# Attention with an MLP behind it: loads of two head pairs in one transfer, rests in eight, a start from two queues, and a new order

## The chip, the cores and the metric

The kernel runs on one core of one Trainium2 chip. The metric is the device time of one execution in microseconds (us), the median of several runs. A kernel under test and the kernel before run in the same rounds on the same chip. A ratio is the mean time of one kernel's fast runs over the mean time of the other's fast runs of the same rounds, so it is not quite the ratio of the medians quoted beside it. A span in a profile is about 2 us shorter than the time of its run.

## The reference, cut to what matters

```python
# q, k, v: (8 batches, 12 heads, 448 tokens, 64), f32
q_n, k_n = rmsnorm(q, g_q), rmsnorm(k, g_k)
attn = softmax(q_n @ k_n.T / sqrt(64)) @ v          # per batch and head
x = attn.transpose(0, 2, 1, 3).reshape(3584, 768)
h = x @ w_in                                        # 768 x 2048
out = (h * clip(h + 3, 0, 6) / 6) @ w_out           # 2048 x 768
```

448 tokens are three tiles of 128 and a rest of 64. Two heads make a pair; a batch has six pairs and there are 48 in all.

## The kernel before

The program first collects all its operations in a list, with the engines that may do each, and then emits them in a fixed order, a table of numbers found by a search. Each engine works through its own instructions strictly in that order. TensorE (PE) does the scores, the values and both matmuls of the MLP; the MLP of one batch fills PE while the attention of the next goes through its chain. SyncE (SP) issues the loads of q, k and v, the transposes done by DMA (`T` of q and k, `xT` of the attention's output) and the stores of the result. The weights are issued by GpSimd (POOL).

The parts that the change touches: loads are issued for each pair, and the 64-token rests for two pairs at a time.

```python
NQK, NV, NVR, ..., NY = 5, 5, 2, ..., 3              # buffers in each ring
qk_r = ring(NQK, [TP, 2 * FULL + 4 * D], FP32, "qk") # q and k of one pair and the rests of two
...
def load(P, want, parts="kqRrvw"):                   # P: the pair
    ...
        if c in "kqv":                               # 128 x 2 heads x 192: 192 KB
            em(nc.sync.dma_start(
                out=dst.rearrange("p (h x) -> p h x", h=2),
                in_=src[b, hs, 0:T * TP].rearrange("h (p t) d -> p h (t d)", t=T)))
        ...
        for n in range(2):                           # even pairs: R (q), r (k), w (v), 64 x 2 x 64: 32 KB
            em(nc.sync.dma_start(out=dst, in_=rows))
...
if P >= NPT:                                         # 13: from here q and k are transposed by DMA, before by PE
    em(nc.sync.dma_start_transpose(out=dst[...], in_=qks[...]))
```

The softmax here doesn't subtract the row's maximum and nothing guards it: scores larger than these inputs give would overflow.

## Time and profile before

| | kernel before |
|---|---|
| time, median (lowest to highest) | 462.8 us (462.6 to 463.7) |
| span in the profile | 461.1 us |
| PE busy / idle | 423.9 / 37.2 us |
| PE idle before 60, in 100 to 260, in the rest | 15.1 / 17.2 / 4.9 us |
| issues of loads of q, k and v | 288 |

The table is read from the windows that the prediction shows: a stretch's length less PE's busy time in it is PE's idle time, and only PE's idle time or a low clock can be gained, because PE is the fullest engine. The prediction mentions the list of PE's waits in the third stretch without showing it. Here it is; the columns are the instruction's line, what it waited for, the sum in us, how often, and the longest.

```profile
PE X L715 <- ACT eT L680: 3.6, 3, 2.0
PE S L690 <- ACT eT L680: 2.7, 4, 1.5
PE M L769 <- DVE gT L786: 2.1, 2, 2.0
PE X L670 <- DVE xn L732: 2.0, 3, 0.8
PE M L769 <- DMA xT<-xn: 1.7, 2, 1.0
PE M L806 <- DVE gT L786: 1.6, 2, 1.5
PE M L769 <- ACT y L816: 1.1, 2, 0.7
```

Nearly every line names ScalarE (ACT) or VectorE (DVE), and none names SP. The chain of waits, whole span:

```profile
PE 48%; DMA 7%; SPq 4%; DVE 3%; POOL 2%; ACT 1%; issue 1%; ACTq 0%; POOLq 0%; DVEq 0%
```

There the transfers and SP's queue follow PE, ahead of DVE and ACT.

### The profile page before, as it was taken

The page shows a single profiled execution, that of the slowest core. Times are in us where ns is not written, and L with a number is a line of the kernel's source. Part 1 is how long each engine was busy: PE and PEld are TensorE (multiplying, and loading weights), DVE is VectorE, ACT ScalarE, POOL GpSimd, SP SyncE. Part 2 cuts the span into 40 slices and gives each one's busy share as a digit, 9 for nine tenths or more (in the row PEclk, how much of TensorE's full clock was granted, in tenths as well). Part 3 has the DMA queues.
Part 4 walks back from the last instruction along what each step waited for, and adds up shares of the span by engine and source line. Part 5 has one row for each costly group of instructions (what it writes and reads, how often), then busy time and mean ns, then how long its engine had stood idle before and what let it go on. Part 6 is the DMA issues. An engine that isn't in the chain of part 4 may idle for free.

```text
span 461.1 us, 9700 instructions
## 1 busy us (share of the span) xinstructions
PE 423.9 (92%) x3629; PEld 246.4 (53%) x3629; DVE 279.5 (61%) x644; ACT 253.6 (55%) x486; POOL 161.8 (35%) x264
## 2 busy tenths in 40 slices
PE   8486899999889897999898999999999999999996
PEld 8243655554544454554454555555555565555554
DVE  5479587458687565866675477675568645345130
ACT  3488677768866654457665856664463433312110
POOL 4456863096464454462633333134040000000000
PEclk9769799999999999899999999999999999999999
DMA  6888999757866767677789767755144411120112
GB/s 163 175 167 181 238 222 225 185 158 193 152 140 151 190 147 197 143 167 200 189 156 192 193 154 144 138 151 146 32 99 96 94 47 31 29 80 1 68 36 103
DMA packets 123699, 64.25 MB, mean 139 GB/s; under 512 B 77828, under 2 KB 120196, under 8 KB 123652
## 3 DMA queue, kind: packets, MB, share of 16 engines
q1 hardware_dynamic: 118256, 57.24, 51.4%
q0 software_dynamic: 5248, 6.29, 8.7%
q8 instruction: 28, 0.46, 0.4%
q14 instruction: 19, 0.16, 0.1%
q10 hardware_dynamic: 148, 0.10, 0.1%
HBM read 45.61 MB, written 11.01 MB: 123 GB/s over the span
## 4 chain that ended last, share of the span: by engine, by line
PE 48%; DMA 7%; SPq 4%; DVE 3%; POOL 2%; ACT 1%; issue 1%; ACTq 0%; POOLq 0%; DVEq 0%
PE M L806 17%; PE M L769 15%; PE X L715 4%; PE S L806 4%; DMA qk<-in_k_dram 3%; DMA qk<-in_q_dram 2%; PE S L670 2%; PE X L769 1%; SPq L457 1%; SPq L602 1%; POOL sq L488 1%; PE S L769 1%; ACT eT L680 1%; DMA T<-qko 1%; SPq L438 1%
## 5 line engine op out<-in xcount | busy, mean ns | idle before, releaser
L769 PE MATMUL M<-xT,w_in_sb 128*128 128x448 bf16 x714 | 156.8, 355 | 5.7 <-DVE gT L786 2.3
L806 PE MATMUL M<-w_out_sb,gT 128*128 128x384 bf16 x752 | 136.9, 326 | 1.6 <-DVE gT L786 1.6
L680 ACT ACTIVATE eT<-S 128x896 bf16<-128x896 f32 x114 | 102.0, 915 | 41.3 <-PE S L670 41.1
L806 PEld LDWEIGHTS <-gT 128*128 128x128 bf16 x912 | 86.3, 98 | 62.9 <-issue 10.1
L769 PEld LDWEIGHTS <-w_in_sb 128*128 128x128 bf16 x768 | 71.3, 98 | 73.3 <-issue 19.1
L786 DVE SCALAR_TENSOR_TENSOR gT<-ts,M 128x448 bf16<-128x448 f32 x119 | 73.5, 619 | 33.5 <-ACT ts L780 30.9
L495 DVE TENSOR_REDUCE ssq<-sq 128x12 f32<-128x768 f32 (+4 forms) x51 | 52.3, 1027 | 33.1 <-POOL sq L488 24.5
L488 POOL TENSOR_TENSOR sq<-qk 128x384 f32<-128x384 f32 (+2 forms) x49 | 44.7, 917 | 64.6 <-DMA qk<-in_q_dram 26.2
L715 PEld LDWEIGHTS <-eT 128*128 128x128 bf16 x1152 | 45.8, 99 | 22.5 <-issue 7.0
L782 DVE TENSOR_SCALAR ts<-M 128x448 f32<-128x448 f32 x73 | 45.2, 621 | 18.4 <-PE M L769 18.1
L715 PE MATMUL X<-va,eT 128*128 128x65 bf16 x1152 | 49.5, 196 | 6.2 <-ACT eT L680 3.9
L486 ACT ACTIVATE sq<-qk 128x384 f32<-128x384 f32 (+1 forms) x48 | 27.5, 574 | 36.9 <-DMA qk<-in_q_dram 21.6
L528 POOL TENSOR_TENSOR qke<-qk,rs 128x384 bf16<-128x384 f32 x45 | 36.8, 825 | 26.5 <-ACT rs L503 20.4
L780 ACT ACTIVATE ts<-M 128x448 f32<-128x448 f32 x46 | 25.0, 546 | 38.2 <-PE M L769 37.3
L528 POOL TENSOR_TENSOR qko<-qk,rs 128x384 bf16<-128x384 f32 x44 | 35.6, 827 | 17.5 <-DMA T<-qko 8.4
L670 PE MATMUL S<-T 64*128 64x448 bf16 x228 | 35.3, 372 | 2.7 <-ACT eT L680 1.9
L732 DVE TENSOR_TENSOR xn<-X,rd 128x512 bf16<-128x512 f32 x48 | 33.2, 691 | 5.1 <-DMA xT<-xn 3.2
L819 DVE TENSOR_SCALAR y<-M 128x384 f32<-128x384 f32 x27 | 14.9, 553 | 26.7 <-PE M L806 26.6
L694 ACT ACTIVATE eR<-S 128x448 bf16<-128x448 f32 x48 | 26.4, 550 | 6.7 <-PE S L690 6.7
L680 ACT ACTIVATE eT<-X 128x896 bf16<-128x896 f32 x30 | 27.4, 915 | 0.0
L670 PEld LDWEIGHTS <-T 64*128 64x128 bf16 x288 | 11.1, 94 | 26.9 <-issue 19.9
L399 POOL CAST va<-vf 128x384 bf16<-128x384 f32 x19 | 9.6, 503 | 42.8 <-PE X L715 22.0
(84 smaller groups left out, 351.2 us busy)
## 6 DMA issues: line engine op xcount, KB each, us to landing
qk<-in_k_dram SPq DMA_DIRECT2D x48, 192.0 KB, 2.8
qk<-in_q_dram SPq DMA_DIRECT2D x48, 192.0 KB, 3.2
vf<-in_v_dram SPq DMA_DIRECT2D x48, 192.0 KB, 3.1
out_dram<-y SPq DMA_DIRECT2D x23, 384.0 KB, 2.5
w_in_sb<-in_moe_w_in_dram POOLq DMA_DIRECT2D x4, 768.0 KB, 9.8
w_out_sb<-in_moe_w_out_dram POOLq DMA_DIRECT2D x4, 768.0 KB, 8.5
out_dram<-y SPq DMA_DIRECT2D x9, 192.0 KB, 2.8
qk<-in_q_dram SPq DMA_DIRECT2D x48, 32.0 KB, 2.8
```

Of the source, the lines that this page charges most:

```text
L486: em(nc.scalar.square(out=o, in_=x))
L488: em(nc.gpsimd.tensor_tensor(out=o, in0=x, in1=x, op=A_MULT))
L495: em(nc.vector.tensor_reduce(out=ssq[:, c0:c1], in_=sq[:, c0 * D:c1 * D].rearrange("p (n d) -> p n d", d=D), axis=AX_X, op=A_ADD))
L528: em(nc.gpsimd.tensor_tensor(out=qks[:, b0:b0 + T].rearrange("p t h d -> p h t d"), in0=x, in1=rs[:, c0:c0 + 2 * T].rearrange("p (h t) -> ...
L670: em(nc.tensor.matmul(out=ps[:, a, 0:S], lhsT=qkT[r, k0:k0 + TP], rhs=qkT[r, q0:q0 + S], start=True, stop=True))
L680: em(nc.scalar.activation(out=eT[:, t, PAD:PAD + S2].rearrange("p (a s) -> p a s", a=2), in_=ps[:, :, 0:S], func=EXP, bias=0.0, scale=1.0))
L715: em(nc.tensor.matmul(out=X_ps[:, i // 2, o:o + (E1 if t < T else 2 * E1)], lhsT=eT[:, t, c0:c0 + TP] if t < T else eR[:, c0:c0 + TP], rhs ...
L732: em(nc.vector.tensor_tensor(out=xn[:].rearrange("p (a i) h d -> p a (i h) d", a=2), in0=xv[:, :, :, 0:D], in1=rd[:].unsqueeze(3).to_broad ...
L769: em(nc.tensor.matmul(out=ps[:, 0:S], lhsT=w_in_sb[:, kt, f * 128:(f + 1) * 128], rhs=xT[:, kt, x0:x0 + S], start=(kt == 0), stop=(kt == N ...
L782: em(nc.vector.tensor_scalar(ts[:], ps[:, 0:S], -3.0, 3.0, A_MAX, A_MIN))
L786: em(nc.vector.scalar_tensor_tensor(out=gT[:, f, e * S:(e + 1) * S], in0=ts[:], scalar=lim, in1=ps[:, 0:S], op0=op, op1=A_MULT))
L806: em(nc.tensor.matmul(out=ps[:, 0:nc0], lhsT=gT[:, f, i * 128:(i + 1) * 128], rhs=w_out_sb[:, f, c0:c0 + nc0], start=(f == 0), stop=(f == ...
```

## The change

Its intent is to take issues off SP: q of two pairs comes in one transfer of 384 KB, and so do k and v; the rests of a whole batch come in eight transfers (four for q, two each for k and v) instead of eighteen. The buffers are cut to match: three double ones for six pairs, and two for y instead of three. At the start, q of the first pair and the first rests go out from ACT's queue while SP sends k. Two more pairs are transposed by DMA, and the order and the choice of engines were searched again. The core of the diff:

```diff
-    NQK, NV, NVR, ..., NY = 5, 5, 2, ..., 3
-    qk_r = ring(NQK, [TP, 2 * FULL + 4 * D], FP32, "qk")
+    NQK, NRR, ..., NY = 3, 2, ..., 2
+    qk_r = ring(NQK, [TP, 2, 2, FULL], FP32, "qk")
+    rr_r = ring(NRR, [TP, 2, H // 2, D], FP32, "rr")
 ...
-    NPT = 13
+    NPT = 11
 ...
+    def load(P, want, parts="kqv", n=1, first=False):
+            def fn(e, dst=dst, src=src):
+                em((nc.scalar if e == ACT else nc.sync).dma_start(
+                    out=dst.rearrange("p o (h x) -> p (o h) x", h=2),
+                    in_=src[b, hs, 0:T * TP].rearrange("h (p t) d -> p h (t d)", t=T)))
+    def load_rest(b, want, parts, m0, m1, first=False):
+        ...                                     # R: four transfers, r and w: two each, for pairs m0 to m1
+                em((nc.scalar if e == ACT else nc.sync).dma_start(out=dst, in_=rows))
 ...
+    load(0, -70.0, "q", first=True)             # first=True: from ACT's queue
+    load_rest(0, -69.0, "Rr", 0, 1, True)
+    load(0, -70.0, "k")
 ...
-            load(P + 4, at(P + 4) - 30.0)
+            elif P % 2 == 0:
+                load(P + 4, at(P + 4) - 30.0, n=2)
+            if (P + 4) % NPAIR == 0:
+                load_rest((P + 4) // NPAIR, at(P + 4) - 30.0, "Rrw", 0, NPAIR // 2)
 ...                                            # ORDER (2349 numbers) and the choice of engines: new
```

## The prediction

> **What bounds the kernel now.** I began with the page's busy shares. PE works 92% of the span, so a gain has to come from PE's idle time or from low-clock time, and I cut the span into stages by windows.
>
> ```profile
> PE 423.9 (92%) x3629; PEld 246.4 (53%) x3629; DVE 279.5 (61%) x644; ACT 253.6 (55%) x486; POOL 161.8 (35%) x264
> ...
> 0.00:60.00 60.00, 44.89 (x468) 31.25 (x469) 39.46 (x158) 37.07 (x76) 35.02 (x71) 0.83 0.87 185
> 60.00:100.00 40.00, 38.93 (x344) 22.37 (x342) 25.02 (x53) 29.89 (x61) 17.79 (x27) 1.00 0.87 189
> 100.00:260.00 160.00, 142.85 (x1266) 79.00 (x1266) 108.82 (x226) 103.42 (x207) 82.15 (x123) 0.99 0.75 173
> 260.00:300.00 40.00, 39.81 (x347) 22.65 (x344) 27.01 (x56) 26.01 (x51) 11.80 (x18) 1.00 0.74 158
> 300.00:420.00 120.00, 120.00 (x976) 68.39 (x974) 69.64 (x138) 49.80 (x77) 15.00 (x26) 1.00 0.31 77
> 420.00:461.00 41.00, 37.44 (x240) 22.73 (x237) 9.56 (x16) 7.46 (x15) 0.00 (x0) 1.00 0.17 59
> ```
>
> Columns: stretch, its length, busy us of PE, PEld, DVE, ACT, POOL, granted clock, DMA share, GB/s. PE idles 15.1 us before 60 (part of the rest at a clock of 0.83), 1.1 in 60 to 100, 17.2 in 100 to 260, 0.2 in 260 to 300, nothing in 300 to 420, 3.6 in the tail: 37 in all. Only the first and the third stretch have something to give.
>
> For the third I asked what PE waits for. Its list has no big item (exponentials 6.8 us, xn 2.9, gT 3.7, a transposed xT 1.7), and neither ACT (65%) nor DVE (68%) is full. So I looked at what feeds them, the queue of SP, which the page does not count as an engine.
>
> ```profile
> 112.73 0.61 SPq L457 DMA_DIRECT2D vr<-in_v_dram  x1
> 113.39 0.59 SPq L438 DMA_DIRECT2D qk<-in_q_dram  x1
> 114.03 0.61 SPq L457 DMA_DIRECT2D qk<-in_q_dram  x1
> 114.68 1.30 SPq L602 DMA_TRANSPOSE T<-qko  x1
> 116.15 1.29 SPq L602 DMA_TRANSPOSE T<-qke  x1
> 117.48 0.66 SPq L438 DMA_DIRECT2D vf<-in_v_dram  x1
> 118.19 0.63 SPq L457 DMA_DIRECT2D qk<-in_k_dram  x1
> 118.92 0.91 SPq L457 DMA_DIRECT2D qk<-in_q_dram  x1
> 119.93 1.23 SPq L739 DMA_TRANSPOSE xT<-xn  x1
> ```
>
> Start and length of each issue: one begins as the last ends. Adding up these lengths over all of 100 to 260 gives 150 of 160 us (37.0, 38.2, 37.3, 37.3 in the four quarters), against 22.5 of 40 in 60 to 100 and 32.4 of 40 in 260 to 300. PE is idle where SP is full, and hardly elsewhere. SP issues in order: a transpose that PE needs stands behind loads that nobody needs yet, and the reverse. The chain of waits runs through just that: issue, transfer, square, reduction, issue.
>
> ```profile
> 168.38 0.63 SPq L457
> 169.07 0.59 SPq L830
> 169.70 0.60 SPq L457
> 170.35 2.16 DMA qk<-in_k_dram
> 172.58 1.05 POOL sq L488
> 173.65 1.23 DVE ssq L495
> ```
>
> The start is another stage. PE first stalls on the 64-row rest of k (pair 0), whose loads stood tenth and thirteenth in the queue. Its real work starts at 19.8.
>
> ```profile
> 19.11 0.40 PE L633 MATMUL M<-identity,qke 128*128 128x128 bf16 x2 [3.48 <-POOL qke L554]
> ```
>
> From the first exponential at 20.4 to the end of the sixth pair's last one at 49.1, ACT sets the pace: I count 26.9 us of its instructions in these 28.7 us (17 exponentials of 128x896 at 0.915 and six of 128x448 at 0.55 alone are 18.9). The MLP's matmuls, the filler that makes PE full, begin at 53.
>
> **The Trainium skill.** "DMA: Bandwidth & Descriptors", section Issuing engines are not separate DMA queues, says that issuing from several engines saves only the sequencer's time to start the transfers, "usually small relative to the DMA itself". One issue here is small (0.6 us against 2.8 to 3.2 to landing), but 197 of them in a row fill 94% of SP. "Perfetto Trace Analysis", section DMA Instruction — HWDGE, says that the length shown is the wait for the descriptor generator, its use and the sequencer's semaphore push, not the movement of data. So the lengths above are SP's own occupancy, and fewer issues free it even if all bytes stay. "TensorE: Matmul & The Clock Gate", Part 1, says that the array falls to half clock after an idle window of about 3.4 us and needs as long a busy one to come back. The trace agrees: after the stall of 3.48 us the granted clock is 0.50 from 18 to 30.
>
> **The change part by part.** Loads on SP: six pairs now take 18 of 192 KB (0.53 us each) and 18 of 32 KB (0.62): 9.5 + 11.2 = 20.7 us. Afterwards 9 of 384 KB and 8 rest transfers. If the length of an issue depends little on its size, that is 9 x 0.53 + 8 x 0.62 = 9.7 us. This is an estimate; for it speaks that 64x2x64, with 128 runs, takes 0.62 and 128x2x192, with 256 runs, 0.53. In 100 to 260 there are 149 load issues; 17/36 of them is 70, so 79 x 0.57 = 45 us leave SP, and its 150 become 105, or 71% of a shorter stage: between the 56% and 81% of the two neighbours, which lost 1.1 and 0.2 us. At 1.1 per 40 us, the 17.2 of idle become 4.3, a gain of 12.9. But PE's own list names ACT and DVE, whose work the change does not reduce. Some of those gaps are theirs whatever SP does, so I count 11.
>
> The start: q of pair 0 and the rests of q and k go out from ACT while SP sends the two k. In the order of instructions the first scores stand before the k rest, so the 3.48 us stall leaves the path of the first score, and part of the dummy matmuls stands between the first scores and should hold the clock. With the data landed by about 7 and the known steps after it (reduction 0.7, two rs 0.4, scaling about 2, transposing and copying 1.2) the first exponential comes at about 13, an estimate. But ACT then has to work off 36.3 us of instructions up to the sixth pair's last exponential (32.4 before, counted in both orders with the durations of this trace), of which 4.8 are done by then: 13 + 31.5 x 28.7/26.9 = 46.6 against 49.1. Seven microseconds of earlier start shrink to 2.5. Some of ACT's extra (one exponential of 0.9, casts) is later work done early, so I count 3.
>
> PE: 15 fewer transposes (99 to 84, as pairs 11 and 12 go to DMA) at about 0.1 us each: 1.5, on the path because PE is full. For it SP has two more issues of 1.3. PE's other counts are the same: 768 + 912 MLP matmuls, 1344 for the values.
>
> Added and off the path: even pairs from the second on take three squares instead of two; 58 of 825 ns and 14 smaller ones make POOL's squares about 56 us instead of 45, on an engine that is 51% busy in the full stage. ACT's fall from 27.5 to 24. One y buffer less: a row block of y takes PE 32 x 0.163 = 5.2 us and its store lands after about 3, so two suffice. Bytes and run lengths stay, so the DMA share stays near 0.75. Sum: 11 + 3 + 1.5 = 15.5, so 462.8 becomes 447.3.
>
> **The rivals.** First, ACT and DVE are the real bound of 100 to 260. PE's list speaks for it, and the new order pulls pairs 10 to 18 forward with less filler (I count 44.5 us of PE, 46.6 of ACT, 44.9 of DVE). Against: before, the same pairs took 54.9 us from exponential to exponential though no engine had over 48.5 of work, while SP was full. If it holds, the stage gives 5 and the time is about 454. Second, an issue's length grows with what it carries: 384 KB then cost 1.06 and the large rests up to three times 0.62. SP would get back some 30 of its 45 us, the gain would be 4 and the time 455. The equal lengths of unequal forms speak against it. Third, larger transfers land later, and one awaited piece now waits for twice its bytes; with buffers for six pairs of inputs that should be covered, but where it isn't it costs some 3 us at the start: 450. Fourth, the searched order fits the chip better than I count, the start keeps its seven and the stage loses its 17 nearly whole: 440.
>
> **Range and chances.** The central sum is 447.3. The fourth rival sets the lower edge at 440, the first and half the second the upper at 454.5. Faster by over 2% means under 453.6; only the first two rivals, near their full size, keep it above: 0.81. Same 0.17. Slower needs a new stall of over 9 us beside a freed SP: 0.02.
>
> **What would show it.** SP's lengths in about 100 to 250 should fall to some 70%, with double loads at 0.5 to 0.7 each. PE's idle there should be 4 to 8 us and the gaps named after xT gone. The first exponential should stand near 13, the sixth pair's last near 47, the clock before 60 above 0.83. PE's transposes should be 84. I am wrong if SP is free and PE still idles 12 us or more (first rival), if double loads show over 0.9 us (second), or if PE waits for transfers of q and k before 60 (third).

## The result, and the profile after

The changed kernel took 439.38 us (438.18 to 440.0, 4 runs) against 462.75 for the kernel before in the same rounds: ratio 0.9487, 95% interval 0.9464 to 0.9511. That is faster, as the prediction thought likely, but 8 us faster than its central value and just below the lower edge of its range.

The changed kernel's page and windows (stretch, length, busy us of PE, PEld, DVE, ACT, POOL, granted clock, DMA share, GB/s):

```profile
PE 416.4 (95%) x3614; PEld 241.3 (55%) x3614; DVE 277.8 (63%) x644; ACT 248.0 (57%) x484; POOL 171.2 (39%) x287
...
0.00:60.00 60.00, 43.65 (x489) 30.14 (x490) 38.56 (x159) 41.19 (x89) 38.86 (x79) 0.89 0.95 215
60.00:100.00 40.00, 38.88 (x358) 21.78 (x356) 28.89 (x65) 28.55 (x61) 18.93 (x31) 1.00 0.92 209
100.00:260.00 160.00, 159.76 (x1402) 88.59 (x1401) 123.70 (x252) 110.66 (x222) 91.52 (x140) 1.00 0.83 187
```

PE is idle for 0.24 us of the 160 from 100 to 260, where it was idle for 17.15. Its idle time over the whole span fell from 37.2 to 21.2. PE's list of waits for that stretch has one line left, and the chain of waits has neither DMA nor SP:

```profile
PE M L786 <- DVE gT L803: 0.2, 1, 0.2
```

```profile
PE 82%; DVE 7%; ACT 2%; issue 1%; DVEq 0%; ACTq 0%
```

SP's own queue in the changed kernel has gaps by the second half of the stretch (start, length of the issue), where it had stood end to end before:

```profile
195.22 1.96 SPq L619 DMA_TRANSPOSE T<-qke  x1
197.23 1.29 SPq L619 DMA_TRANSPOSE T<-qko  x1
198.75 1.19 SPq L756 DMA_TRANSPOSE xT<-xn  x1
203.29 0.36 SPq L847 DMA_DIRECT2D out_dram<-y  x1
203.76 1.32 SPq L619 DMA_TRANSPOSE T<-qke  x1
```

In these lines no load stands between the transposes, and SP stands idle from 200 to 203.3.

The spans differ by 461.1 - 437.6 = 23.5 us. Of these 16.0 are PE's idle time (16.9 less in 100 to 260, 1.2 more before 60, 0.3 less elsewhere) and 7.5 are PE's busy time. The fifteen transposes that left PE are about 1.5 of the 7.5, at the prediction's 0.1 us each. In 180 to 220 the clock rose from 0.96 to 1.00, which is 0.04 x 40 = 1.6. The rest, some 4, I put down to the higher clock before 60 (0.83 to 0.89) without having measured it apart.

### The profile page after: what moved, and what is told of

Same layout as the page of the kernel before. It is cut to its first block, busy times and chain, and to the rows that moved or that the text cites. A ratio compares the mean times of both kernels' runs of the same rounds, so it can differ in the third digit from the quotient of the medians.

```text
span 437.6 us, 9478 instructions
## 1 busy us (share of the span) xinstructions
PE 416.4 (95%) x3614; PEld 241.3 (55%) x3614; DVE 277.8 (63%) x644; ACT 248.0 (57%) x484; POOL 171.2 (39%) x287
## 2 busy tenths in 40 slices
DMA packets 123377, 64.71 MB, mean 148 GB/s; under 512 B 77508, under 2 KB 119876, under 8 KB 123332
## 4 chain that ended last, share of the span: by engine, by line
PE 82%; DVE 7%; ACT 2%; issue 1%; DVEq 0%; ACTq 0%
PE M L786 29%; PE M L823 27%; PE X L732 9%; PE S L687 6%; PE S L823 5%; PE S L707 2%; DVE gT L803 2%; DVE ssq L512 1%; DVE xn L749 1%; ACT eT L697 1%; DVE ts L799 1%; PE X L823 1%; PE X L687 1%; PE X L786 1%; PE X L766 1%
## 5 line engine op out<-in xcount | busy, mean ns | idle before, releaser
L697 ACT ACTIVATE eT<-S 128x896 bf16<-128x896 f32 x124 | 110.8, 917 | 44.7 <-PE S L687 39.4
L799 DVE TENSOR_SCALAR ts<-M 128x448 f32<-128x448 f32 x69 | 42.9, 622 | 36.3 <-PE M L786 34.1
L502 POOL TENSOR_TENSOR sq<-qk 128x384 f32<-128x384 f32 x58 | 47.3, 824 | 31.0 <-DVE ssq L512 13.1
L732 PEld LDWEIGHTS <-eT 128*128 128x128 bf16 x1152 | 47.6, 100 | 13.9 <-issue 2.2
L797 ACT ACTIVATE ts<-M 128x448 f32<-128x448 f32 x50 | 27.3, 546 | 37.6 <-PE M L786 29.6
L687 PE MATMUL S<-T 64*128 64x448 bf16 x248 | 38.0, 365 | 3.0 <-DVE T L606 1.6
L833 ACT ACTIVATE y<-M 128x384 f32<-128x384 f32 x24 | 11.8, 490 | 36.2 <-PE M L823 36.0
L836 DVE TENSOR_SCALAR y<-M 128x384 f32<-128x384 f32 x23 | 12.8, 555 | 29.9 <-PE M L823 29.9
L500 ACT ACTIVATE sq<-qk 128x384 f32<-128x384 f32 x38 | 19.4, 522 | 7.6 <-DMA qk<-in_k_dram 4.1
L823 PE MATMUL S<-w_out_sb,gT 128*128 128x384 bf16 (+1 forms) x128 | 22.1, 316 | 0.1
```

The costliest lines, as they stand in the source:

```text
L502: em(nc.gpsimd.tensor_tensor(out=o, in0=src, in1=src, op=A_MULT))
L687: em(nc.tensor.matmul(out=ps[:, a, 0:S], lhsT=qkT[r, k0:k0 + TP], rhs=qkT[r, q0:q0 + S], start=True, stop=True))
L697: em(nc.scalar.activation(out=eT[:, t, PAD:PAD + S2].rearrange("p (a s) -> p a s", a=2), in_=ps[:, :, 0:S], func=EXP, bias=0.0, scale=1.0))
L732: em(nc.tensor.matmul(out=X_ps[:, i // 2, o:o + (E1 if t < T else 2 * E1)], lhsT=eT[:, t, c0:c0 + TP] if t < T else eR[:, c0:c0 + TP], rhs ...
L797: em(nc.scalar.activation(out=ts[:], in_=ps[:, 0:S], func=RELU, bias=3.0, scale=1.0))
L799: em(nc.vector.tensor_scalar(ts[:], ps[:, 0:S], -3.0, 3.0, A_MAX, A_MIN))
```

## The experiments

Two theories stood. **A**: SP's occupancy by issues makes PE idle, so anything that takes issues off SP gains, and the names ACT and DVE in PE's list are only who stood last in a chain that SP had delayed. **B**: something else in the change does it: the larger transfers themselves, or the new order, which could have removed the idle time without the merging. Later the number of small transfers, apart from the time that their issues take of SP, joined B.

### Splitting the loads again, in the new order

In the changed kernel, every merged load is sent as single-pair transfers, at its place in the order (only the rests of q stay at four a batch). `e1_split_all` splits both kinds, `e2_split_big` only the first block, `e3_split_rest` only the second.

```diff
-                em((...).dma_start(out=dst.rearrange("p o (h x) -> p (o h) x", h=2), in_=...))
+                for i in range(n):
+                    em((...).dma_start(out=dst[:, i].rearrange("p (h x) -> p h x", h=2), in_=...[pair i]))
 ...
-                    em((...).dma_start(out=dst, in_=rows))
+                    for i in range(1 if c == "R" else m1 - m0):
+                        d, s = (dst, rows) if c == "R" else (dst[:, 2 * i:2 * i + 2], rows[:, 2 * i:2 * i + 2])
+                        em((...).dma_start(out=d, in_=s))
```

> The changed kernel with its order, but every merged load split again at its place: 34 load issues for six pairs instead of 17 (before had 36). Theory A (fewer issues free SP, and that removed PE's idle time): the idle time between 100 and 240 comes back by 10 us or more, and the time is 452 to 462. Theory B (the new order removed it, the merging is secondary): within 3 us of the changed kernel, 437 to 442.

> Only the transfers of two pairs of heads are split (18 + 8 issues for six pairs). A: nine more issues of 0.5 us in six pairs, about a half of the loss of the full split, 443 to 451. B: within 3 us of the changed kernel.

> Only the 64-row rests of k and v are split, by head pairs (9 + 16 issues). A: eight more issues of 0.6 us, again about half of the loss, 443 to 451. B: within 3 us of the changed kernel.

Measured: all split 470.78 us (ratio to before 1.0149, interval 1.0104 to 1.0194); only the large ones 444.9 (0.9591; median of its three fast runs, the fourth was slow); only the rests 459.81 (0.9907). Theory A had the direction right and the sizes wrong: 470.8 and 459.8 lie above the ranges that it gave (452 to 462, 443 to 451). The new order without the merging is slower than the kernel before, so the order alone is not the gain; it needs a short queue on SP. The chain of waits of the run with all split, and its list of PE's waits in 140 to 260:

```profile
PE 50%; SPq 12%; DMA 11%; POOL 11%; DVE 7%; issue 5%; ACT 2%; POOLq 0%; DVEq 0%; ACTq 0%
```

```profile
PE S L690 <- DVE T L607: 6.7, 1, 6.7
PE M L789 <- DMA xT<-xn: 5.8, 2, 5.5
```

SP's queue is now second in the chain, and the first wait is put down to DVE although it is a transposed tile that DVE could only scale once SP had issued its transpose:

```profile
152.53 1.91 SPq L466 DMA_DIRECT2D vr<-in_v_dram  x3
154.47 0.60 SPq L466 DMA_DIRECT2D rr<-in_q_dram  x1
155.18 1.32 SPq L622 DMA_TRANSPOSE T<-qke  x1
```

```profile
159.58 0.93 PE L690 MATMUL S<-T 64*128 64x448 bf16 x4 [6.70 <-DVE T L607]
```

The last write to qke had ended at 142.5. From 144.7 to 155.1 SP sent fifteen issues of loads end to end, then this transpose, which landed at 158.6. That is how the names in PE's list mislead.

Splitting the rests costs 20 us and splitting the large loads about 5.5, though they add nearly the same number of issues (8 and 9 a batch). The rests' issues are longer, and in the middle they add 27 us to SP's time, the large loads' 21 (table below). A split rest also goes out as a burst of three issues (six where both halves follow each other), and I suppose that such a burst in front of a transpose costs more than pairs of issues do. That was not tested.

### Merging the loads in the old order

`e4_old_order_merged` has the changed kernel's loads and buffers, but the order and the choice of engines of the kernel before, mapped operation by operation; a merged load stands where the first of its parts stood, or later where its buffer isn't free. The first loads are those of the kernel before, all on SP. With three y buffers it doesn't fit the memory, so it has two. `e4c_before_two_y` is its control: the kernel before with two y buffers and nothing else.

```diff
-NQK, ..., NY = 5, ..., 3        # e4c: this line alone
+NQK, ..., NY = 5, ..., 2
```

> The kernel before, in its own order, way choices and first loads, with the merged transfers from the fifth pair of head pairs on (a merged load stands where the first of its parts stood, or as early as its buffer allows; two y buffers). A: the idle time of 17 us in 100 to 260 falls to 4 to 6, time 447 to 452. B: it stays above 12 us, time 457 to 464.

> The kernel before with two y buffers instead of three and nothing else. This is a control for the run that merges the loads in the old order, which also had to lose a y buffer. If two buffers suffice, as the prediction said: 462 to 465 us, within 0.5% of the kernel before. If the store of y holds its buffer back, PE idles more after 300 us and the time is 466 or more; then the run with the old order undersold the merging by as much.

Measured: 446.59 us (0.9621, interval 0.9577 to 0.9665), just under what theory A gave, and for the control 465.99 (1.0056, interval 1.0011 to 1.01). The control falls at the border of its two expectations: two y buffers cost the old order perhaps half a per cent. (Its clock before 60 us was 0.74, as in e4, against 0.83 for the kernel before; why is open.) The merging alone is worth 0.9621 / 1.0056 = 0.957, an estimate of 20 us, because the two ran on different chips. PE's list in 100 to 260 with the old order and merged loads:

```profile
PE M L784 <- DVE y L834: 3.2, 2, 2.0
PE M L784 <- ACT y L831: 1.1, 1, 1.1
PE S L685 <- ACT eT L695: 0.5, 1, 0.5
```

PE's idle time there is 160 - 154.78 = 5.2 us, of which 4.3 are waits for y. The waits for exponentials (6.8 before), xn (3.1) and gT (3.7) shrank to 0.7, 0.2 and nothing, although ACT and DVE do the same work in the same order. Nearly all of them had been SP's.

### The same small transfers from another engine, in the old order

`e8_rest_from_pool` is the kernel before with its order and its unmerged transfers; only the issuer of k's and v's rests changes, from the second batch on (12 of 36 load issues per batch).

```diff
-                    em(nc.sync.dma_start(out=dst, in_=rows))
+                    em((nc.gpsimd if P >= NPAIR and c in "rw" else nc.sync).dma_start(out=dst, in_=rows))
```

> The kernel before, unmerged and in its own order, but the rests of k and v (12 of the 36 load issues for six pairs) are issued by POOL from the second batch on. Theory A (what hurts is SP's occupation by issues): SP loses 7.4 us of issues in six pairs, PE's idle time in 100 to 260 falls from 17 to 6 to 11 and the time to 450 to 458, unless POOL, which pays for them, becomes the new wait. Rival (what helps is that transfers are larger, not that SP issues fewer): no gain, 461 to 466.

Measured: 445.53 us (0.9609, interval 0.957 to 0.9648). Nothing is merged, no order is new, and three quarters of the change's gain is there (464.27 - 445.53 = 18.7 us of the 25.0 that the changed kernel gained on the same chip), more than the 450 to 458 us expected. The transfers are as many and as small as before, and the transposes land no sooner (medians 3.4 and 3.6 us against 3.0 and 3.4), so here the transfers' number and size are not the cause. Theory A holds without any part of the change but the freed SP:

```profile
100.00:260.00 160.00, 157.24 (x1422) 88.68 (x1420) 120.72 (x250) 116.74 (x231) 121.85 (x188) 1.00 0.86 196
```

```profile
PE X L749 <- DVE xn L732: 1.4, 1, 1.4
PE S L670 <- ACT eT L680: 0.5, 1, 0.5
PE M L769 <- DVE gT L786: 0.5, 1, 0.5
```

PE idles 2.8 us, and again the waits named after ACT and DVE are gone. POOL pays for it: 121.9 us busy in this stretch against 82.2.

### The small transfers from GpSimd, in the new order: two misses

Would the run with all split recover in the same way? `e10_split_pool` lets GpSimd issue its split rests of k and v, `e11_split_pool_late` only from the third batch on.

```diff
-                        em((nc.scalar if e == ACT else nc.sync).dma_start(out=d, in_=s))
+                        em((nc.scalar if e == ACT else nc.sync if c == "R" else nc.gpsimd).dma_start(out=d, in_=s))
 # e11: ... nc.sync if c == "R" or b < 2 else nc.gpsimd
```

> The changed kernel with every load split again, as in the run that split all, but the split 64-row rests of k and v issued by GpSimd: the same small transfers and the same order, of 34 load issues per six pairs 12 leave SP. If SP's occupancy is what made the run with all split slow (470.8 us), most of its loss over the changed kernel comes back: 442 to 450 us, near the 446.3 of the run that keeps 26 load issues on SP; PE idle between 100 and 260 us falls from about 20 to under 6. If the many small transfers themselves are the cause (their number in the DMA queues, their landing), it stays at 460 or more whoever issues them.

> The changed kernel with all loads split, the rests of k and v issued by GpSimd from the third batch on only, so that the start has GpSimd as free as in the changed kernel. If SP's occupancy in the middle is what the split costs: PE's idle time between 100 and 260 us falls from 18.9 (all split, all on SP) to under 7 with the start like that of all split, and the time is 452 to 458 us. If the number of small transfers is the cause: 466 or more, with idle over 14.

Measured: 466.14 us (1.0065, interval 1.001 to 1.012) and 463.31 (0.9995, interval 0.9953 to 1.0037), against the 442 to 450 and the 452 to 458 that theory A had made me expect. Both are misses. PE's idle time between 140 and 260 us did fall as A says, from 17.7 with all on SP to 4.5 in both. But before 140 it rose from 24.1 to 33.3 and 32.5. In the first of the two, POOL is busy for 227 us of the whole span instead of 171, its loads stood 6.1 us behind transfers of weights, and PE waits at the start for POOL:

```profile
PE M L653 <- POOL qke L574: 10.3, 2, 8.1
PE X L408 <- DVE g_t L403: 5.5, 1, 5.5
```

In the second, POOL waits in its own order (list of POOL's waits, 20 to 140 us), and every load behind it waits too:

```profile
POOL qke L548 <- ACT rs L523: 15.6, 4, 5.9
POOL sq L505 <- issue: 6.6, 1, 6.6
POOL vb L393 <- PE X L735: 5.1, 1, 5.1
```

So in this order most of what SP won is lost on POOL. The old order bore such issues although POOL was about as busy there (121.9 us in 100 to 260, against 124.4 and 122.4 here); why is open. The two runs leave the question open that they were to settle for the new order: is it SP's occupancy, or the small transfers?

### SP's occupancy by itself

`e13_tiny` leaves the changed kernel's transfers and order alone and adds loads of four bytes that nobody reads: one behind each double load, two behind each rest of three pairs. `e14_tiny_twice` adds twice as many.

```diff
+    scr_t = const.tile([128, 3], FP32, name="scr_t")     # e14: 6 columns
+    def tiny(n):
+        for _ in range(n):                               # e14: 2 * n
+            c, p = divmod(len(used), 128)
+            used.append(p)
+            em(nc.sync.dma_start(out=scr_t[p:p + 1, c:c + 1], in_=k[0, 0, 0:1, 0:1]))
 ...
+                tiny(n - 1)                              # behind a load of q, k or v
+                    tiny(0 if c == "R" else m1 - m0 - 1) # behind a rest
```

> The changed kernel, transfers and order untouched, with 104 added loads of four bytes each on SP, which nobody reads: one behind each double load, two behind each rest load of three pairs, so SP has as many issues as in the run with all split, and no more data. If SP's occupancy is what costs: the added issues (0.5 us each, some 30 us in 100 to 260) bring SP back to about 146 of 160 us and the time toward that run's 470.8: 455 to 472. If the split transfers themselves cost: 438 to 442, PE idle under 2 us between 100 and 260.

> The same with 208 added loads of four bytes. If occupancy costs, SP is full from 60 to 260 us and falls behind: 485 to 520. If it doesn't, under 445. If an issue of four bytes turns out to be much shorter than 0.5 us, this run is the one that has the occupancy of the run with all split: then 455 to 472 here and less in the other.

Measured: 456.22 us (0.9844, interval 0.9785 to 0.9903) and 486.63 (1.0496, interval 1.0451 to 1.054). The trace counts 130 and 260 added loads, not the 104 and 208: I had counted program rows that held several issues. 130 is exactly the number of issues by which the run with all split exceeds the changed kernel (274 against 144).

```profile
L306 SPq DMA_DIRECT2D scr_t<-in_k_dram x130: 219/350/614, 3.7 to 310.6; - x130
```

Issues that carry nothing cost 17 us, and twice as many 47 (by the ratios, as the changed kernel did not run on that chip). The 130 loads add 261 packets to 123,377; the split of all loads adds 2,081.

Two things besides SP's time are in these figures. First, `e14_tiny_twice` has an edit that was not meant: the doubled count also went into the dummy matmuls at the start. They take 18.8 us of PE instead of 11.5, and the first exponential comes at 18.0 instead of 15.3. So 47 is not the price of the loads alone. Second, in the trace SP's issues take eight semaphores in turn (375 issues on eight in `e13_tiny`), and all but the first few wait for their own one, that is for the landing of a transfer mostly eight issues back. A tiny load takes a place too, and at the start SP waited for landings, in `e13_tiny` for 17.2 us before 60 (2.4 in the changed kernel). The two longest kinds:

```profile
SPq L306 <- DMA rr<-in_q_dram: 4.6, 2, 3.1
SPq L437 <- DMA qk<-in_k_dram: 4.2, 2, 3.1
```

From 100 to 260 such waits are 0.3 us in `e13_tiny`, 3.8 in `e14_tiny_twice`, and none in the kernel before, the changed one, and those with all loads or the rests split. So what SP's time costs is read in the middle.

The runs side by side, there. A fixed window holds more work in a faster run, so I take the stretch from the 41st to the 101st of the 144 exponentials that write eT. In the new order it holds 41 transposes by DMA in every run. SP's times are sums of the lengths of its issues, without the gaps:

| kernel | SP in loads, us | SP in all issues, us | PE idle, us | the stretch, us | time, us |
|---|---|---|---|---|---|
| changed | 42 | 107 | 0.0 | 151.0 | 439.4 |
| changed, large loads split (e2; the profiled run took 447.8) | 64 | 125 | 6.0 | 159.8 | 444.9 |
| changed, tiny loads (e13) | 69 (27 tiny) | 129 | 8.0 | 163.8 | 456.2 |
| changed, rests split (e3) | 69 | 132 | 11.2 | 167.3 | 459.8 |
| changed, all split (e1) | 83 | 147 | 18.7 | 176.5 | 470.8 |
| changed, twice the tiny loads (e14) | 87 (46 tiny) | 149 | 26.6 | 187.1 | 486.6 |
| before | 87 | 149 | 16.4 | 168.1 | 462.8 |
| old order, merged (e4) | 40 | 104 | 3.2 | 149.8 | 446.6 |
| before, k and v rests on POOL (e8) | 53 | 112 | 0.8 | 147.6 | 445.5 |

In the new order (the first six rows) the stretch grows with SP's time in loads, whether the added issues carry split loads or nothing. So 12.8 of the tiny loads' 17 us are lost in this stretch, and 25.5 of the 31 that the split of all loads costs; the rest is lost before it. With equal time on SP, tiny loads and split rests differ by 3.5 us: that much may be due to the transfers themselves, or to where the issues stand. The rows with the old order hold the same number of exponentials, but not just the same work. The two runs with a loaded POOL (45 and 46 us in loads, 10 of idle PE, 163 for the stretch) stand outside the table, since another engine stalled them.

### The start

`a0_after_again`, `a1_after` and `a2_after` are the changed kernel again, beside the runs that they are compared with. `e5_one_queue`, and again `e9_one_queue_again`, send its first loads from SP's queue too; `e6_k_first` has k's reduction, rescaling and transposes of the first pair before q's in the order; `e12_k_first_one_queue` is both.

```diff
 # one queue, in load and in load_rest
-                em((nc.scalar if e == ACT else nc.sync).dma_start(
+                em(nc.sync.dma_start(
 # k first: ORDER, the first pair
-    gains, ... q: reduce, ln, exp, scale, transposes, copy ... k: the same ...
+    gains, k: reduce, ln, exp, scale, transposes, copy ... q: the same ...
```

> The changed kernel itself, as the yardstick for the others of this call on the same chip: ratio to before 0.945 to 0.953.

> The changed kernel with the first loads (q of pair 0 and the rests of its q and k) issued by SP like all others, at their places. If the second queue is what helps the start, five issues of 0.5 to 0.6 us now stand ahead of the next loads, the first exponential comes 1 to 3 us later than 15.9 and the time is 1 to 3 us longer. Rival: the start is paced by ACT's work up to the sixth pair, so the time stays within 1 us.

> The changed kernel with only the order of the first pair's steps changed: the gain factors and k's reduction, scaling, transposes and copy before q's, as k lands first (its square ends at 4.3, but its reduction waits behind q's until 9.4). The first score should come at 12 to 13 instead of 15.2. If the first score sets the start, the time falls by 2 to 3 us, to about 437; if ACT's load up to the sixth pair sets it, by 0 to 1.5.

> The changed kernel with its first loads on SP's queue alone, again, with more rounds and beside the unchanged changed kernel on the same chip. The first time it took 438.2 us against 439.3. If the second queue hurts at the start: again 1 to 2 us below the changed kernel, first exponential about 2 us earlier. If that was noise: the two within 0.5 us of each other.

> The changed kernel itself, again, for comparison with the run beside it: 439.3 us, within 0.5%.

> The changed kernel with its first loads on SP's queue alone and k's preparation of the first pair before q's: the two start experiments together. One queue alone took 436.9 and 438.2 us, k first alone 439.5 (the changed kernel 439.1 to 439.3). If the start is set by when k's data and rescaling are ready: the first exponential before 13.5 and 435 to 437 us. If the wait for q's share on GpSimd takes its place as it did with two queues: 437 to 439.

> The changed kernel itself on the same chip as the two runs beside it: 439.3 us, within 0.5%.

| kernel | time, us | ratio to before | first exponential, us |
|---|---|---|---|
| changed, beside e5 and e6 (a0) | 439.27 | 0.9475 | 15.4 |
| one queue (e5) | 438.19 | 0.9454 | 13.6 |
| k first (e6) | 439.46 | 0.9476 | 16.4 |
| changed, beside e9 (a1) | 439.12 | 0.9484 | 15.3 |
| one queue, again (e9) | 436.91 | 0.9440 | 13.5 |
| changed, beside e12 (a2) | 439.50 | 0.9481 | 15.5 |
| k first and one queue (e12) | 436.05 | 0.9421 | 13.9 |

The second queue does not help. With one queue, the first exponential is 2 us earlier both times, and the time 1 to 2 us lower, though the intervals of the two kernels overlap each time. The stall that PE has in the changed kernel instead of the old one is for the gain factors, whose own small load is on ACT's queue as well:

```profile
PE X L408 <- DVE g_t L403: 4.9, 1, 4.9
```

With the first loads on SP's queue this wait is 2.3 to 2.4 us (e9, e5), so I take the loads beside the factors' to lengthen it. k first alone gains nothing and has its first exponential at 16.4 (the first score had been expected at 12 to 13), because PE then stands before q's share, scaled by POOL:

```profile
PE M L646 <- POOL qke L541: 3.4, 1, 3.4
```

Both together are not stopped by that wait; the longest before 60 us are then waits for xn and T, which belong to the work itself. At 436.05 us (435.8 to 438.13, six runs, against 438.01 to 440.48 of the changed kernel on the same chip) this version is the fastest: 0.9421 / 0.9481 = 0.994 of the changed kernel.

## Why the prediction was right or wrong

**That SP bounds the middle: right.** The tiny loads, the split loads, and the old order with merged loads or with rests moved to GpSimd show it from several sides. The intent of the change was read correctly, and so was its direction.

**The size of the middle: wrong, and this is the step that failed.** The prediction had worked out a gain of 12.9 us for 100 to 260, and then cut it to 11 because "some of those gaps are theirs whatever SP does", ACT's and DVE's. The stage gave 16.9 us of PE's idle time, and 1.6 more of clock. Next to nothing of the gaps was ACT's or DVE's: with the order unchanged and SP freed, in two different ways (e4, e8), the waits for exponentials, xn and gT shrank from 13.6 us to 0.9 and 2.4. The first rival, that ACT and DVE are the bound, has fallen with them. The undiscounted 12.9 was too low as well, as it took the idle time of the less loaded neighbour stage as a floor: 4.3 us of idle time were to remain and 0.2 did.

**SP at 70% of the stage: right as a mean, not in form.** Its issues last 115 of the 160 us (145 before, without the gaps that the prediction counted in its 150), and 107 of the 151.0 us in the table, 71%. Loads gave back 43 us of the 45 expected. But it is not even: 91% and 89% in the two quarters to 180, then 57% and 50%. PE did not idle even in the full quarters, where it had idled 8.7 us before with SP at 91%. So fullness of SP is not itself the stall; I take it that what counts is whether a transpose or load that PE waits for stands behind issues that could have come later. The lines of the run with all split show one such case.

**The length of an issue: right.** The large loads' medians stayed at 0.54 to 0.55 us with twice the bytes, those of the rests at 0.61 to 0.63 with up to three times:

```profile
L438 SPq DMA_DIRECT2D qk<-in_k_dram x48: 367/530/1050, 0.8 to 303.3; - x48
L457 SPq DMA_DIRECT2D qk<-in_k_dram x48: 595/607/1472, 6.0 to 292.5; - x48
```

```profile
L428 SPq DMA_DIRECT2D qk<-in_k_dram x25: 368/552/2520, 0.8 to 267.6; - x25
L463 SPq DMA_DIRECT2D rr<-in_k_dram x16: 595/616/2768, 4.3 to 214.6; - x16
```

The first two lines are of the kernel before, the last two of the changed one (lowest, median and highest ns). The second rival has fallen. The third, that larger transfers land later, is true of the landing (4.4 to 4.7 us against 2.8 to 3.2 for the large loads) but no wait of PE in the middle came of it.

**The start: the sum about right, the steps not.** The first exponential came at 15.9 instead of 13, since the wait for the gain factors took the place of the one removed, and the sixth pair's last exponential began at 49.9 (48.5 before) where 46.6 was predicted for its end. In return the clock was higher and PE had done more of other work. PE's idle time before 60 grew by 1.2 us and its clock rose from 0.83 to 0.89; the 3 us of the prediction are not refuted by that, nor shown. The two queues that were to bring the gain bring none. The prediction's reading of the clock there is loose: in the kernel before, the clock had fallen to 0.50 by 18, while the stall of 3.48 us lasted to 19.1, and it stayed at 0.50 from 22 to 26 with PE busy for 3.7 of 4 us; no run here tests the idle window of 3.4 us.

**Transposes: right in number.** 84 instead of 99; their 1.5 us were not measured apart.

**Two y buffers suffice: right in the new order**, where no wait for y is left in the middle, but not in the old one, where they took 4.3 us of e4's middle.

**The fourth rival**, that the searched order fits better than counted and the stage loses its 17 us nearly whole, came true at its own figure of 440, by its part on the stage; that the start keeps its seven is not shown. It was the lower edge of the range, and it deserved more than a tail. It is not the order alone, though: with the merging and the old order the time was 446.6, with the order and no merging 470.8. The last 7 us need both, except for the 2 to 3 that two y buffers may cost the old order. (The parts of the first and second rival add up to 453.3 and 454.3, not 454 and 455; it changes nothing here.)

## What to carry to other kernels

Add up the lengths of the issues on the queue that feeds everything before believing the names in the busiest engine's list of waits: a wait belongs to the engine that came last, not to the one that made it late. To measure what an issuing queue's occupancy costs, add transfers of a few bytes to it, look in its list of waits for landings that they add, and check that nothing else was edited. Moving issues to another engine pays only where that engine's own order can bear them, and an order searched for a short queue can be worse than the old one when the queue grows long again.

## What the Trainium skill lacked or had wrong

- "DMA: Bandwidth & Descriptors", section Issuing engines are not separate DMA queues, calls the sequencer's time to start a transfer "usually small relative to the DMA itself". For a single transfer that agrees here (0.53 us against 2.8 to 3.2 to landing). The section does not speak of the sum, and there it can matter: 130 added issues of four bytes cost 17 us of the kernel's time, and moving a third of the load issues to another engine gained 18.7 us with all transfers left as they were.
- The same section does not give the length of one issue by kind. On SP the medians were 0.53 to 0.55 us for 192 and for 384 KB, 0.61 to 0.63 for 32 to 96 KB of rests, 0.35 for four bytes (0.25 in the run with twice as many), and 1.2 to 1.3 for a transpose.
- "Perfetto Trace Analysis", section DMA Instruction — HWDGE, counts waiting and the use of the descriptor generator into an issue's length. The runs show how long that can get: in the changed kernel's start, where the DMA share was above 1.1 (28 to 44 us), rest issues that else take 0.6 us took up to 7.2.

```profile
28.23 0.59 SPq L428 DMA_DIRECT2D vf<-in_v_dram  x1
28.91 7.24 SPq L463 DMA_DIRECT2D vr<-in_v_dram  x1
36.25 2.77 SPq L463 DMA_DIRECT2D rr<-in_k_dram  x1
```

- No page that I read says what a small load issued by GpSimd costs GpSimd: 0.61 to 0.63 us of its time for 32 KB (medians), as much as the issue takes of SP.
- No page gives the spread of a whole kernel's mean granted clock over runs: on one chip, eight fast runs of the kernel before had a mean clock of 0.96 to 0.98 and spans of 459.6 to 463.8 us, so that differences under 1% need several runs.
